# A fused attention and gated-MLP kernel on one core: the last projection in seven quads of seven products, and the second gate's weight blocks by way of a DRAM scratch

## The chip, the cores and the metric

The kernel runs on one core of a Trainium2 chip. The metric is device time in microseconds (us) for one execution. The engines are named as in the profile: PE multiplies matrices, DVE (vector), ACT (scalar) and POOL do elementwise work, SP issues transfers, and each works through its own queue in order. Matrix results land in eight PSUM banks of 128x512 numbers, which DVE and ACT read.

## The reference, cut to what matters

Two layers on a sequence of 2048 tokens of width 1024. The first (a chunked attention) is untouched by the change. The second is this:

```python
def _B_ref(x, w_in, w_sp, b_sp, w_out):          # x: 2048 x 1024, F = 3584, Fh = 1792
    z = _gelu(x @ w_in)                          # w_in: 1024 x 3584
    z1 = z[..., :Fh]
    z2 = _layernorm(z[..., Fh:])
    g = einsum('ts,bsf->btf', w_sp, z2) + b_sp[None, :, None]   # w_sp: 2048 x 2048
    return einsum('bsf,fd->bsd', z1 * g, w_out)  # w_out: 1792 x 1024
h  = x + A(layernorm(x))
h2 = h + _B_ref(layernorm(h), ...)
```

The product of `w_sp` and `z2` is called the gate. The product with `w_out` is the last projection; its result is added to `h`.

## The kernel before

The program is written as one long list of operations per engine. A small recorder (`_Recorder`, all operations issued at line L210) derives the semaphore waits between engines from the addresses that operations read and write. So the order on each engine is the order of the Python code, and nothing is rescheduled.

Several products are made by Strassen's scheme in Winograd's form: a product of 2x2 blocks by seven block products in place of eight, with sums of blocks on DVE ahead of them and sums of results afterwards. `SUMS` names the four derived weight blocks t1 to t4: t1 = b12 - b11, t2 = b22 - t1, t3 = b22 - b12, t4 = b21 - t2.

The part that matters here is the last third, from about 483 us on.

- **First gate**, `gate(0, ...)`: output tokens 0 to 1023. Seven groups g = 0 to 6. A group is seven products of eight matmuls of 128x512 each (names t2, t1, b11 for a later group, t3, b21, t4, b22 in the order on PE). The products t2, t3 and t4 pile up in one bank, and between them DVE must read the sum so far (`u2` after t2, `u3` after t3, `VB` after t4), so t3 waits for `u2` and t4 waits for `u3`. Between those reads DVE also makes the four sums `SS` for the next products (`s_sum`). `copy1` (ACT) takes b11's product to `s1`, and POOL adds the bias rows (`s1b2`, `s1b1`). The callbacks `each(g, k)` place other work at four points of a group.
- **Plain units**: 16 of them between the gates. A unit is 14 matmuls with `w_out` for 128 tokens by 512 columns, one addition on DVE (`fin`) and a store. They cover tokens 0 to 1023, which the first gate has just finished. Meanwhile 16 transposing transfers bring the second gate's blocks of `w_sp` (`sp_load(1, ...)`), DVE scales them to 16-bit floats and forms t1 to t4, and ACT takes sums of squares for the scales.
- **Second gate**, `gate(1, each=each1)`: tokens 1024 to 2047. Its `each1` places the work on the blocks of `w_out` (`ob_scale` on ACT, 16 `ob_sum` pieces on DVE).
- **Last projection in quads**: four groups, each seven products of seven matmuls for two chunks of 128 tokens by 1024 columns, that is what four plain units do. They cover tokens 1024 to 2047.

Of the kernel before, what the change touches and what calls it, by code (L numbers as in the profile page):

```python
# [33 lines left out]
class _Recorder:  # L34
# [52 lines left out]
    def record(self, eng, name, args, kw, dma=None):  # L87
# [94 lines left out]
        if dma is not None:  # L182
            self.dmas.append(op)
            if any(self.cells_of(a)[0] == "dram" for a in aps_out):
                self.out_dmas.append(op)
            sb = [a for a in aps_out + aps_in if self.cells_of(a)[0] == "sbuf"][0]
            key = (aps_out[0] is sb, sb.tensor.name, int(sb.offset))
            sem = self.dma_sems.get(key)
            if sem is None:
                sem = self.dma_sems[key] = [self.nc.alloc_semaphore("d%d" % len(self.dma_sems)), 0]  # L190
            sem[1] += 16
            op.val = sem[1]
            op.dma = sem[0]
# [65 lines left out]
def bass_sequential_preLN__memory_aug_infini_attn__mixer_gmlp__prompt_kernel(  # L259
# [141 lines left out]
    SQB = b3("sqb", [128, 28], BF16)  # L401
# [13 lines left out]
    WO1 = [tens("w_out1%d" % i, [128, 7, 512], BF16, o * K) for i, o in enumerate((30, 190))]  # L415
    WO0H = [tens("w_out0h%d" % i, [128, 7, 512], F16, o * K) for i, o in enumerate((54, 198))]
    FIN2 = tens("fin2", [128, 4, 2, 2, 512], BF16, 14 * K)
    OT4 = [[tens("ot%d%d" % (i, k), [128, 512], F32, (o + 2 * k) * K) for k in range(4)] for i, o in enumerate((38, 118))]
    SY = [tens("sy%d" % i, [128, 4, 7, 128], F16, o * K) for i, o in enumerate((4, 126))]
    FIN = [tens("fin%d" % i, [128, 512], BF16, o * K) for i, o in enumerate((37, 197, 12, 13))]  # L420
# [765 lines left out]

    def sp_load(pr, k, j):
        r0, c0 = 1024 * pr + (512 if k in ("b12", "b22") else 0), 1024 if k in ("b21", "b22") else 0
        sp.dma_start_transpose(RAW[k][:, :, j * 128:(j + 1) * 128],
                               B_w_sp[r0 + j * 128:r0 + (j + 1) * 128, c0:c0 + 1024])  # L1190
# [29 lines left out]
    def prod(b, a, w, first):  # L1220
        for i in range(8):
            pe.matmul(bank(b), a[:, i, :], BH[w][:, i, :], start=(first and i == 0), stop=(i == 7),
                      skip_group_check=True)

    def gate(pr, seam=lambda: None, mid=lambda: None, each=lambda g, k: None):
        inv, zo = (INV[0], Z1T) if pr == 0 else (INVY, Z1X)
        t1, t2 = slice(1024 * pr, 1024 * pr + 512), slice(1024 * pr + 512, 1024 * pr + 1024)
        s1, s1b1, s1b2, u2, u3 = (TMP[k][:] for k in ("s1", "s1b1", "s1b2", "u2", "u3"))
# [26 lines left out]
        pool.tensor_tensor(s1b2, s1, BROW[1][:], ALU.add)  # L1255
        pool.tensor_tensor(s1b1, s1, BROW[0][:], ALU.add)
        p1(1)
        if not pr:
            p1(2)
# [3 lines left out]
        for g in range(7):  # L1263
# [10 lines left out]
            if 1 - pr <= g <= 3:  # L1274
                p1(g + 2)
# [160 lines left out]
    for i in range(2):  # L1436
        sp.dma_start(WO0[i][:], wout[:, 7 * i:7 * i + 7, 0:512])

    units = [(tc, 0, 512) for tc in range(6)] + [(tc, 512, 512) for tc in range(8)] + [(tc, 0, 512) for tc in (6, 7)]
# [8 lines left out]

    def z1_norm(g, k):
        for h in range(k and 2):  # L1450
            r, o = 2 * g + (k > 2), 1024 + 512 * h
            if k != 2:
                act.activation(bank(7), Z1T[:, r, o:o + 512], ACTF.Square, accum_out=SQY[:, 2 * r + h:2 * r + h + 1])

    gate(0, seam, mid, z1_norm)
    pool.tensor_copy(TW[:], TOT[:])
    fin_load(units[0], act)
    fin_load(units[1], act)
    for k in ("b11", "b12", "b22", "b21"):
        for j in range(4):  # L1460
            sp_load(1, k, j)
    brow_load(1, act)
    for i in range(2):
        act.dma_start(WO1[i][:], wout[:, 7 * i:7 * i + 7, 512:D])
    pool.tensor_copy(SQB[:], SQY[:])

    def total(n):
        b = next_bank()
        pe.matmul(PS[:, b, 0:n], ONES[:], SQB[:, 0:n], start=True, stop=True)
        dve.tensor_reduce(out=TOT[:], in_=PS[:, b, 0:n], axis=mybir.AxisListType.X, op=ALU.add)  # L1470
        dve.tensor_single_scalar(TOT[:], TOT[:], 1e-30, ALU.max)
# [6 lines left out]
    def scale_y():  # L1478
        total(28)
        pool.tensor_single_scalar(TW[:], TW[:], float(2 * T * FH), ALU.mult)  # L1480
        for k in range(2):
            pool.tensor_tensor(TW[:], TW[:], BSQ[:, k:k + 1], ALU.add)
        pool.tensor_tensor(TOT[:], TOT[:], TW[:], ALU.mult)
# [5 lines left out]
    def brow_sq():  # L1489
        for k in range(2):  # L1490
            act.activation(BH["t4"][:, k, :], BROW[k][:], ACTF.Square, scale=float(np.sqrt(2.0)), accum_out=BSQ[:, k:k + 1])

    def wo_norm(k):
        v = (WO0, WO1)[k // 4][k // 2 % 2].rearrange("p c n -> p (c n)")[:, 1792 * (k % 2):1792 * (k % 2) + 1792]
        act.activation(BH["t4"][:, 0:4, :].rearrange("p c n -> p (c n)")[:, 0:1792], v, ACTF.Square, accum_out=SQY[:, k:k + 1])

    def scale_w():
        total(8)
        power(SCW)
        dve.tensor_tensor(INVO[:], YS[:], SCW[:], ALU.mult)  # L1500
        dve.reciprocal(INVO[:], INVO[:])

    for n, u in enumerate(units):
        if n + 2 < 16:
            fin_load(units[n + 2], act)
        out_unit(u, (lambda i: WO0[i // 7][:, i % 7, :]) if u[1] == 0 else
                 (lambda i: WO1[i // 7][:, i % 7, :]), act)
        if 1 <= n <= 8:
            wo_norm(n - 1)
        if n == 6:  # L1510
            brow_sq()
        if n == 7:
            scale_y()
        if n == 10:
            pool.tensor_copy(SQB[:, 0:8], SQY[:, 0:8])
        if n == 1:
            sp_half("b11")
        if n == 4:
            sp_half("b12")
            sp_sum("t1")  # L1520
        if n == 6:
            sp_half("b22")
            sp_sum("t3")
        if n == 8:
            sp_sum("t2")
        if n == 10:
            sp_half("b21")
            sp_sum("t4")
        if n == 12:
            scale_w()  # L1530
        if n == 13:
            for k in range(1, 4):
                s_sum(k, 0)

    OB = {"b11": WO0H[0], "b21": WO0H[1], "b12": Z1X[:, 0:7, 0:512], "b22": Z1X[:, 7:14, 0:512],
          "t1": Z1X[:, 0:7, 512:1024], "t2": Z1X[:, 7:14, 512:1024], "t3": Z1X[:, 0:7, 0:512]}

    def ob(k, i):
        if k == "t4":
            return Z2H[:, 4 * (i % 4):4 * (i % 4) + 4, 896 * (i // 4):896 * (i // 4) + 128]  # L1540
        return OB[k][:, i, :]

    def ob_scale(k, h):
        src = {"b11": WO0[0], "b21": WO0[1], "b12": Z1T[:, 0:7, 0:512], "b22": Z1T[:, 7:14, 0:512]}[k]
        s = slice(4 * h, 4 + 3 * h)
        act.activation(OB[k][:, s, :], src[:, s, :], ACTF.Copy, scale=SCW[:])

    def ob_sum(o, h):
        a, b = SUMS[o]
        s = slice(h, min(h + 2, 7))  # L1550
        if o == "t4":
            n = 4 * (s.stop - s.start)
            t = 4 * (h % 4)
            dve.tensor_tensor(Z2H[:, t:t + n, 896 * (h // 4):896 * (h // 4) + 128].rearrange("p (c m) n -> p c m n", m=4),
                              OB[a][:, s, :].rearrange("p c (m n) -> p c m n", m=4),
                              OB[b][:, s, :].rearrange("p c (m n) -> p c m n", m=4), ALU.subtract)
            return
        dve.tensor_tensor(OB[o][:, s, :], OB[a][:, s, :], OB[b][:, s, :], ALU.subtract)

    def y_blk(i, j, g, lo=0, hi=7):  # L1560
        t = 1024 + 512 * i + 128 * g
        return Z1X[:, 7 * j + lo:7 * j + hi, t:t + 128]

    def y_sum(k, g, lo=0, hi=7):
        y = SY[g % 2]
        o = y[:, k - 1, lo:hi, :]
        a, b, op = {1: (y_blk(1, 0, g, lo, hi), y_blk(1, 1, g, lo, hi), ALU.add),
                    2: (y[:, 0, lo:hi, :], y_blk(0, 0, g, lo, hi), ALU.subtract),
                    3: (y_blk(0, 0, g, lo, hi), y_blk(1, 0, g, lo, hi), ALU.subtract),
                    4: (y_blk(0, 1, g, lo, hi), y[:, 1, lo:hi, :], ALU.subtract)}[k]  # L1570
        (pool if lo else dve).tensor_tensor(o, a, b, op)

    def fin_in(g):
        for i in range(2):
            tc = 8 + 4 * i + g
            sp.dma_start(FIN2[:, g, i, :, :], out2d[tc * 128:(tc + 1) * 128, :].rearrange("p (h n) -> p h n", h=2))

    def fin_out(g, i, j, lo=0, hi=512):
        tc = 8 + 4 * i + g
        sp.dma_start(out2d[tc * 128:(tc + 1) * 128, 512 * j + lo:512 * j + hi], FIN2[:, g, i, j, lo:hi])  # L1580

    def each1(g, k):
        jobs = {(0, 0): [(ob_scale, "b11", 0)], (0, 1): [(ob_scale, "b11", 1)], (0, 2): [(ob_scale, "b12", 0)],
                (0, 3): [(ob_scale, "b12", 1)], (1, 0): [(ob_scale, "b22", 0)], (1, 1): [(ob_scale, "b22", 1)],
# [49 lines left out]
    for x in range(1, 4):  # L1634
        y_sum(x, 0, 6, 7)
# [69 lines left out]
```

## Time and profile before

| what | value |
|---|---|
| median of 3 runs | 747.42 us (746.77 to 747.52) |
| the profiled execution's own time | 747.58 us |
| its span in the profile | 745.9 us |
| PE busy | 738.8 us, 99% of the span |
| DVE, ACT, POOL busy | 595.8, 439.4, 296.1 us |
| granted PE clock | 1.0 all through |

How to read it: the span is from the first to the last instruction of the profiled execution; 1.7 us lie around it. Busy PE time includes overlap of matmuls that follow each other, so what a matmul costs is read from start to start. Times inside the trace count from the span's start. A row of the timeline gives start, duration, engine, line, operation, output and inputs, shape and count, and in brackets how long the engine sat idle before and what released it.

### The profile page before, as it was taken

To read this page: it belongs to the slowest core of one execution; us is meant where nothing else is said; L and a number is where in the kernel's file an instruction comes from. 1 tells how busy PE (TensorE), PEld (TensorE's weight loads), DVE (VectorE), ACT (ScalarE), POOL (GpSimd) and SP (SyncE) were. 2 spreads that over 40 slices of the span, in tenths; PEclk is the share of its full clock that TensorE was granted. 3 is DMA by queue.
4 is the path that set the end of the run, shared out by engine and by line. 5 is a ranking of instruction groups with operands and counts; after the bars stand their busy time and mean duration, and the time that the engine had idled before them with its cause. 6 is when DMAs were issued, how large, how long until landed. Compare 5 with 4: busy or idle time off the path is not lost.

```text
span 745.9 us, 13501 instructions
## 1 busy us (share of the span) xinstructions
PE 738.8 (99%) x5419; PEld 353.9 (47%) x5419; DVE 595.8 (80%) x1041; ACT 439.4 (59%) x567; POOL 296.1 (40%) x443
## 2 busy tenths in 40 slices
PE   8999999999999999999999999999999999999998
PEld 4445555445545445545554444444444444444444
DVE  5587889899988989878896777797774485989776
ACT  6777888888887888726876669823330445300000
POOL 2565456555554344110155899531220011222342
PEclk9999999999999999999999999999999999999999
DMA  9655668466645752744050036320029960001211
GB/s 298 178 169 128 139 143 176 128 154 157 172 104 166 244 172 64 180 112 128 29 141 1 1 61 123 75 82 0 1 41 162 238 207 18 1 1 52 68 50 56
DMA packets 139374, 82.41 MB, mean 110 GB/s; under 512 B 98352, under 2 KB 126768, under 8 KB 139312
## 3 DMA queue, kind: packets, MB, share of 16 engines
q1 hardware_dynamic: 131776, 74.48, 39.1%
q10 hardware_dynamic: 7536, 7.08, 3.5%
q8 instruction: 42, 0.69, 0.4%
q14 instruction: 20, 0.16, 0.1%
HBM read 50.08 MB, written 8.39 MB: 78 GB/s over the span
## 4 chain that ended last, share of the span: by engine, by line
PE 93%; DVE 4%; ACT 1%; DMA 1%; issue 0%; POOL 0%; DVEq 0%
PE ps L210 93%; DVE sqz L210 1%; DMA wv<-in_A_wv_dram 1%; DVE stats L210 1%; ACT e L210 0%; DVE hch L210 0%; POOL sz L210 0%; DVE tm L210 0%; DVE otok L210 0%; DVE sq L210 0%; DVE rdm L210 0%; DVE pqk L210 0%; DVE rd L210 0%; DVE etmp L210 0%; ACT qk L210 0%
## 5 line engine op out<-in xcount | busy, mean ns | idle before, releaser
L210 ACT ACTIVATE e<-ps 128x2048 bf16<-128x2048 f32 (+1 forms) x96 | 152.7, 1590 | 21.3 <-PE ps L210 20.6
L210 POOL TENSOR_SCALAR_AFFINE_SELECT e<-e 128x512 bf16<-128x512 bf16 x128 | 90.9, 723 | 123.4 <-ACT e L210 123.2
L210 POOL TENSOR_TENSOR tmp_s1b<-tmp_s,brow 128x512 f32<-128x512 f32 x28 | 36.5, 1306 | 121.7 <-DVE tmp_u L210 63.4
L210 PE MATMUL ps<-xnT,wk 128*128 128x512 bf16 x256 | 60.8, 380 | 0.6 <-ACT v L210 0.4
L210 PE MATMUL ps<-wv,xnT 128*128 128x512 bf16 x256 | 60.0, 381 | 0.7 <-DMA wv<-in_A_wv_dram 0.7
L210 PE MATMUL ps<-xnT,wq 128*128 128x512 bf16 x256 | 60.5, 379 | 0.0
L210 PE MATMUL ps<-wo,oT 128*128 128x512 bf16 x256 | 58.2, 380 | 0.8 <-DVE hch L210 0.8
L210 PE MATMUL ps<-w_out,z1T 128*128 128x512 bf16 x224 | 48.6, 379 | 0.0
L210 PEld LDWEIGHTS ps<-v,e 128*128 128x128 bf16 x1280 | 38.8, 96 | 14.0 <-issue 6.5
L210 ACT ACTIVATE tmp_s<-ps,invy 128x512 f32<-128x512 f32 x7 | 4.8, 687 | 64.0 <-POOL tmp_s1b L210 36.0
L210 PE MATMUL ps<-v,e 128*128 128x33 bf16 x1280 | 42.2, 178 | 0.0
L210 POOL TENSOR_TENSOR sz<-wzh 128x512 f16<-128x512 f16 x28 | 34.0, 1216 | 11.2 <-PE ps L210 11.2
L210 DVE BATCH_NORM_STATS2 zst<-z 128x6 f32<-128x448 bf16 x64 | 38.0, 609 | 0.0
L210 PEld LDWEIGHTS ps<-wo,oT 128*128 128x128 bf16 x256 | 24.0, 98 | 28.6 <-DVE hch L210 1.3
L210 PEld LDWEIGHTS ps<-xnT,wk 128*128 128x128 bf16 x256 | 22.6, 98 | 30.6 <-issue 4.5
L210 DVE TENSOR_TENSOR zt<-ps,zt 128x512 f32<-128x512 f32 x28 | 19.1, 686 | 22.2 <-PE ps L210 19.3
L210 ACT ACTIVATE qk<-ps 128x512 bf16<-128x512 f32 x48 | 28.7, 599 | 12.9 <-PE ps L210 12.9
L210 PEld LDWEIGHTS ps<-wv,xnT 128*128 128x128 bf16 x256 | 23.2, 98 | 27.7 <-DMA wv<-in_A_wv_dram 0.9
L210 PE MATMUL ps<-qk 32*128 32x128 bf16 (+3 forms) x512 | 34.5, 302 | 0.7 <-DVE tm L210 0.5
L210 ACT ACTIVATE tmp_s<-ps,inv 128x512 f32<-128x512 f32 x7 | 4.8, 687 | 50.9 <-POOL tmp_s1b L210 37.9
L210 PEld LDWEIGHTS ps<-xnT,wq 128*128 128x128 bf16 x256 | 23.5, 98 | 22.9 <-issue 0.2
L210 PEld LDWEIGHTS ps<-w_out,z1T 128*128 128x128 bf16 x224 | 21.7, 98 | 26.2
(259 smaller groups left out, 1651.0 us busy)
## 6 DMA issues: line engine op xcount, KB each, us to landing
nb<-in_B_w_in_dram SPq DMA_DIRECT2D x16, 448.0 KB, 4.0
nb<-in_B_w_sp_dram SPq DMA_DIRECT2D x14, 512.0 KB, 4.6
xch<-in_A_x_dram SPq DMA_DIRECT2D x16, 256.0 KB, 4.3
xr<-in_A_x_dram SPq DMA_DIRECT2D x16, 256.0 KB, 4.0
out_dram<-hch SPq DMA_DIRECT2D x16, 256.0 KB, 2.4
wz<-in_B_w_in_dram SPq DMA_DIRECT2D x6, 512.0 KB, 4.6
wo<-in_A_wo_dram SPq DMA_DIRECT2D x1, 2048.0 KB, 8.5
fin<-out_dram ACTq DMA_DIRECT2D x16, 128.0 KB, 3.1
```

What stands on the lines that cost most here:

```text
L210: ins = getattr(e, op.name)(*op.args, **op.kw)
```

## The change

Eight groups of four units' work make up the last projection (2048 tokens by 1024 columns). Before, 16 plain units and four quads did it. After, four plain units (tokens 0 to 255) and seven quads do it: quads 0 to 2 take tokens 256 to 1023, quads 3 to 6 take tokens 1024 to 2047, all behind the second gate. For this the first gate's output for tokens 256 to 1023 is scaled and turned into 16-bit floats on ACT during the second gate, after a sum of squares over it (`y0_norm`, `y0_scale`, `y0_conv`).

The second gate's `w_sp` blocks are transposed during the first gate into six staging tiles, stored to a DRAM tensor `WSPT`, and read back by four plain loads of 1 MB (`q_load`). ACT converts b11, b12 and half of b21, DVE b22 and the other half. The sums of squares over `w_out` and over the first gate's operand move into the first gate. In the second gate the first two bias additions move from POOL to DVE, `ob_load` brings blocks of `w_out` in pieces of 128 columns, and the block sums of `w_out` are placed in other groups.

```diff
+    STG = [tens("stg%d" % i, [128, 8, 128], BF16, o * K) for i, o in enumerate((54, 56, 58, 198, 200, 202))]
+    WSPT = nc.dram_tensor("w_spT", (4, 128, 4, 1024), BF16, kind="Internal").ap()
+    HOME1 = {"b11": 4, "b12": 118, "b22": 46, "b21": 126, "t1": 38, "t2": 22, "t3": 118, "t4": 14}
...
+    def stage_in(n):
+        sp.dma_start_transpose(STG[n % 6][:], sp_rows(1, Q4[n // 4], n % 4))
+    def stage_out(n):
+        sp.dma_start(WSPT[n // 4, :, n % 4, :], STG[n % 6][:].rearrange("p c n -> p (c n)"))
+    def q_load(k):
+        sp.dma_start(RAW1[k][:].rearrange("p j c n -> p j (c n)"), WSPT[Q4.index(k)])
+    def q_conv(k):
+        if k == "b22":
+            dve.tensor_single_scalar(BH1[k][:], RAW1[k][:], SC[0][:], ALU.mult)
+            return
+        if k == "b21":
+            dve.tensor_single_scalar(BH1[k][:, 0:2], RAW1[k][:, 0:2], SC[0][:], ALU.mult)
+        for r in range(2 * (k == "b21"), 4):
+            act.activation(BH1[k][:, r], RAW1[k][:, r], ACTF.Copy, scale=SC[0][:])
+    def q_sum(o):
+        a, b = SUMS[o]
+        dve.tensor_tensor(BH1[o][:], BH1[a][:], BH1[b][:], ALU.subtract)
...
-        pool.tensor_tensor(s1b2, s1, BROW[1][:], ALU.add)
-        pool.tensor_tensor(s1b1, s1, BROW[0][:], ALU.add)
+        for o, k in ((s1b2, 1), (s1b1, 0)):
+            (dve if pr else pool).tensor_tensor(o, s1, BROW[k][:], ALU.add)
         p1(1)
-        if not pr:
-            p1(2)
+        p1(2)
...
+    for n in range(20):
+        if n < 16:
+            stage_in(n)
+        if n >= 4:
+            stage_out(n - 4)
+    w0_load(1)
-    units = [(tc, 0, 512) for tc in range(6)] + [(tc, 512, 512) for tc in range(8)] + [(tc, 0, 512) for tc in (6, 7)]
+    units = [(tc, 512 * h, 512) for h in range(2) for tc in range(2)]
...
+    def each0(g, k):
+        z1_norm(g, k)
+        for h, lo in ((1, 15), (0, 21)):
+            for n in range(14):
+                if 4 * g + k == lo + n // 5:
+                    w_norm(h, n)
+            if 4 * g + k == lo + 2 and h:
+                w0_load(0)
...
+        if (g, k) == (4, 0):
+            total(28, SQY, TOTY)
+        if (g, k) == (6, 0):
+            brow_in(1)
+            q_load("b11")
+            q_load("b12")
+            q_conv("b11")
+        if (g, k) == (6, 1):
+            fin_load(units[1])
+            w1_load(1)
+            q_conv("b12")
+        if (g, k) == (6, 2):
+            brow_in(0)
+            fin_load(units[2])
+            fin_load(units[3])
+    gate(0, seam, mid, each0)
+    q_load("b22")
+    q_load("b21")
...
+    brow_sq()
+    q_sum("t1")
     for n, u in enumerate(units):
...
+        if n == 0:
+            s_sum(1, 0)
+            s_sum(2, 0)
+        if n == 2:
+            scale_y()
+            q_conv("b21")
+            q_sum("t3")
         if n == 1:
+            q_conv("b22")
+    q_sum("t2")
+    s_sum(3, 0)
...
+    NG = 7
+    def tcs(g):
+        return (2 + g, 5 + g) if g < 3 else (5 + g, 9 + g)
...
+    for r in range(14):
+        job(r // 7, (r % 7) // 2, y0_norm, r)
+    for h in range(4):
+        job(2 + (h + 1) // 4, (h + 1) % 4, y0_conv, h)
+        job(3 + (h + 1) // 4, (h + 1) % 4, y_sum, h + 1, 0)
+    job(2, 0, y0_scale)
+    job(0, 0, q_sum, "t4")
+    job(0, 0, scale_w)
+    for r in range(7):
+        job(1, 0, ob_load, "b12", r)
+        job(3, 0, ob_load, "b22", r)
...
+    slots = [(2, 1), (2, 2), (2, 3), (3, 0)] + [(g, k) for g in range(4, 7) for k in range(4)][1:12]
+    for n, (o, h) in enumerate([(o, h) for o in ("t1", "t2", "t3", "t4") for h in range(4)]):
+        if n < len(slots):
+            job(*slots[n], ob_sum, o, h)
...
-    for g in range(4):
+    ob_sum("t4", 3)
+    for g in range(NG):
```

`total(n, src)` puts one small matmul on PE and two small operations on DVE; `power` is one POOL operation and two on DVE. `brow_sq` squares the two bias rows on ACT, `scale_y` scales them. `job(g, k, ...)` puts work at point k of group g of the second gate.

## The prediction

> **What bounds the kernel now.** I read the page first (busy shares, then the chain that ended last), then PE's timeline from the first gate on, then DVE's and ACT's in the same stretch, last the stretches of DMA.
>
> ```profile
> PE 738.8 (99%) x5419; PEld 353.9 (47%) x5419; DVE 595.8 (80%) x1041; ACT 439.4 (59%) x567; POOL 296.1 (40%) x443
> ...
> PE 93%; DVE 4%; ACT 1%; DMA 1%; issue 0%; POOL 0%; DVEq 0%
> ```
>
> PE is never free: a matmul removed is time removed, unless PE then waits for another engine. PE's timeline prices the matmul:
>
> ```profile
> 565.79 1.89 PE L210 MATMUL ps<-b22h,ss 128*128 128x512 f16 x8
> 567.51 24.34 PE L210 MATMUL ps<-w_out,z1T 128*128 128x512 bf16 x112
> 591.69 0.18 PE L210 MATMUL ps<-sqb,ones 128*128 128x28 bf16 x1
> 591.72 15.27 PE L210 MATMUL ps<-w_out,z1T 128*128 128x512 bf16 x70
> ```
>
> 112 matmuls from 567.51 to 591.69 are 0.216 us each; a gate product of eight is 1.726 us from start to start (565.79 to 567.51). The tiny matmul with ones costs PE some 0.03 us. From 482 us on PE shows one late start, 0.08 us:
>
> ```profile
> 674.43 1.28 DVE L210 TENSOR_TENSOR z1x<-z1x 128x1024 f16<-128x1024 f16 x2
> 675.63 0.74 DVE L210 SCALAR_TENSOR_TENSOR tmp_u<-ps,invy,tmp_s1b 128x512 f32<-128x512 f32 x1
> ...
> 674.62 1.89 PE L210 MATMUL ps<-b21h,z2h 128*128 128x512 f16 x8
> 676.43 1.90 PE L210 MATMUL ps<-t4h,z2h 128*128 128x512 f16 x8
> ```
>
> This is the second gate's group 4: two `ob_sum` pieces stand ahead of `u3`, so t4 starts at 676.43 and not at 676.35, 0.06 us after `u3` ends. DVE is the engine that PE will meet when work is moved.
>
> **The gain.** Plain units go from 16 to 4, 12 x 14 = 168 matmuls less; quads from 4 to 7, 3 x 49 = 147 more. 21 matmuls x 0.216 = 4.53 us. The new operands with a stride (four runs of 128 columns) cost nothing extra: the last projection's t4 already reads in such runs, seven matmuls in 1.51 us.
>
> **The staging.** 16 transposes (1.4 us of SP each: four in 5.50) and 16 stores of 256 KB, some 0.75 us of DMA each (at the 335 GB/s shown below), start when the first gate does. At 2.2 us a step they end near 519, with SP's later loads queued behind them; `w_out` lands some 6 us later, near 525. Its first reader is ACT's `w_norm`, which cannot start before 527.8 (`copy1` at 525.65, then two squares). Ten of these at 0.755 us end at 535.3; PE asks for them at 539.9 (`total` writes the bank that the squares use). Price nothing, with 2 us of cover at the load and 4.6 at the matmul; beyond that PE waits one for one. The squares moved into the first gate lie in ACT's idle time (8.5 us ahead of each `copy1`).
>
> **The seam between the gates** is the dear place. Before, 48.4 us of units covered it; now 12.1. A chain begins at 553.90 with ACT's last `copy1` and has no gap:
>
> ```profile
> 553.90 0.69 ACT L210 ACTIVATE tmp_s<-ps,inv 128x512 f32<-128x512 f32 x1 [12.60 <-PE ps L210]
> 554.49 0.59 ACT L210 ACTIVATE ps<-z1T 128x512 f32<-128x512 bf16 x1
> 555.23 0.60 ACT L210 ACTIVATE ps<-z1T 128x512 f32<-128x512 bf16 x1
> ...
> 592.02 2.29 DVE L210 TENSOR_TENSOR t1h<-b12h,b11h 128x4096 f16<-128x4096 f16 x1
> 594.23 1.28 DVE L210 TENSOR_TENSOR fin<-fin,ps 128x512 bf16<-128x512 bf16 x2
> 595.42 1.28 DVE L210 TENSOR_SCALAR b22h<-b22r,sc 128x4096 f16<-128x4096 bf16 x1
> ```
>
> On ACT: `copy1` 0.59 (start to start), 14 `w_norm` at 0.755 = 10.57, eight conversions of 128x1024 (1.14 each in the trace, 1.04 start to start) 8.32, the last one's end 0.10: b12 is ready at 573.5. On DVE from there, from start to start: t1 2.21, fin 0.60, two sums 1.33, fin 0.60, b22 1.31, fin 0.60, the scale's three small ones 0.46, half of b21 0.64, t3 2.21, fin 0.60, t2 2.21, a sum 0.60, the two bias additions 1.28, c11 and its product 1.24, `u2` 0.67, a sum 0.61, t4 2.21, the scale of `w_out` 1.28 (as from 611.88 to 613.16, a trip to POOL in it), `u3` 0.75 and 0.06 to PE. That is 21.47: PE may start t4 of group 0 at 595.0. PE's own work brings it there at 553.70 (`p1(6)`'s end) + eight products 13.81 + units 12.09 + four products 6.90 + four more 6.90 + 0.03 = 593.4. So PE waits 1.57 us here (part of it at t3, for `u2`). The bias additions moved from POOL have no row on DVE; 0.60 to 0.75 each from the f32 additions there, 0.64 taken. Bounds for the seam: 0 (the chain's starts 1.6 earlier in all, over its 40 operations) and 3 (1.5 later). Queued behind `u3` on DVE are `VB` and the next `SS` sums; PE's b22 wants the first, and has 1.7 us for it.
>
> **The second gate.** A group's DVE work is 9.1 us: PE has 12.08 in groups 1 to 3, 10.36 in the others. After t2's end `u3` may start 4.38 us later where no b11 product stands between (three products 5.18, less `u3`'s 0.75 and 0.06), 6.1 with one; else t4 is late.
>
> - Group 2: `y0_scale` has DVE wait for PE's `total`, 3.70 after t2's end. It takes 2.04 (1.66 as from 611.88 to 613.54, and a second pair of small ones 0.38), then one `ob_sum` 0.60: `u3` at 6.34, t4 0.2 late.
> - Group 4: from `u3` to the next `u2` DVE takes 6.45 (675.63 to 682.08). Two `y_sum` pieces there in group 3 put group 4's `u2` at 0.87 after t2's end instead of 0.20. Then, from start to start, `u2` 0.67, sums 0.61, 0.72 and 0.61, `y_sum` 0.60, `ob_sum` 0.60: `u3` at 4.68, t4 0.30 late.
> - Group 5: two `ob_sum` make those 6.45 into 7.65; with 0.81 to PE that is 8.46, where t3 was due 0.81 + 6.90 = 7.71 after the same `u3`: 0.75 late. One and a half more pieces ahead of `u3` put t4 0.09 late. Group 6 has no sums for a next group and makes it up.
>
> Together 1.34 us, bounds 0.4 (today's late start, five times) and 3 (each piece twice as dear). The quads' `sy` addition takes 0.61 alone and 1.58 beside POOL's additions, but POOL's in the gate run beside `VB` reads and end before the next piece. [...]
>
> ACT: 14 `y0_norm` of about 1 us, `ob_scale` (1.99 and 1.56) and eight `y0_conv` pieces of about 1.3 (from the rows of 1024 and 1536) end near 628, 1.4 us ahead of the `y_sum` that wants them; beyond that DVE and PE wait. The 14 `ob_load` of 128 KB go out from 591 on; at the transposes' 180 GB/s seven take 5 us, and ACT asks at 611. Price nothing.
>
> **The quads** add three groups of the form already there, where DVE idles 1.7 us ahead of `u3`'s counterpart; nothing waits.
>
> **The sum.** -4.53 - 0.08 (today's late start, counted anew above) + 0.03 (three `total` for two) + 1.57 + 1.34 = -1.67. From the profiled execution's 747.58 that is 745.9; it lies 0.16 above the median of the runs, 747.42, so 745.8 is my time.
>
> **The rivals.**
>
> *A, all covered.* DVE and ACT keep their places and the gain comes whole: 747.42 - 4.5 = 742.9. For it: hand sums from start to start are tight and small overlaps may help. Against: the seam's chain has no gap and the one late start today is of just this kind.
>
> *B, slower: the scratch comes back late.* From 559.1 (when t2's old block, b11's new home, is free) to the end of b21 one queue holds 5.64 MB: four blocks 4.19, `w_out` 0.92, bias rows and `fin` 0.53. DVE wants b21 at 580.6, 7.1 us into its chain. Two stretches give the rate:
>
> ```profile
> 570.00:573.00 3.00, 3.00 (x16) 1.36 (x14) 0.69 (x1) 0.00 (x0) 0.00 (x0) 1.00 1.22 214
> 601.00:602.00 1.00, 1.00 (x6) 0.48 (x5) 0.00 (x0) 1.00 (x1) 0.78 (x3) 1.00 0.99 335
> ```
>
> (PE, PEld, DVE, ACT, POOL busy, clock, DMA share, GB/s.) Plain loads run at 335, loads among transposes at 214. Data flow some 1.5 us after an issue. At 335 all is in at 559.1 + 1.5 + 16.8 = 577.4; at 214 at 587.0, 6.4 us late, and PE as much: 752.2. It turns slower than before by 0.2% where b21 lands 3.1 us late, at a rate of about 244. For it: 1 KB pieces of bias and `w_out` lie between. Against: no transposes are in that queue.
>
> The profile shows the clock at 1.0 in every stretch. [...]
>
> *C, no change.* The second gate's jobs at their upper bound, 3 us in place of 1.34, the seam as forecast: 747.5.
>
> *Not doing what it says* is excluded for PE: the order of instructions holds 56 unit matmuls and 343 in quads.
>
> **How the numbers follow.** A measurement of this kernel tells about 0.2% (1.5 us) from no change, so my forecast lies on that edge: chance 0.47 for it, of which 0.27 is faster by over 0.2% and 0.20 within. A 0.20 (faster), B 0.20 (slower), C 0.13 (within). Faster 0.47, same 0.33, slower 0.20. The range goes from A's time, 742.9, to 749.0, the lower half of B; the forecast's own is 744.3 to 747.3.
>
> **What would show it.** Right: 56 unit matmuls in one piece of 12.1 us, PE's late starts at t4 of the second gate's group 0 (1.3 to 1.6 us, released by `tmp_u`) and at t3 and t4 of groups 4 and 5, none in the quads. The first step falls if ACT's b12 conversion ends elsewhere than about 6 us after the first gate, the second if DVE idles ahead of group 5's `u2`. Wrong: b21's conversion waiting for DMA, PE waiting at `total` in the first gate, or a clock under 1.0.

## The result, and the profile after

| | before | after |
|---|---|---|
| median of 20 runs each, side by side | 747.79 us (746.77 to 748.95) | 746.46 us (745.68 to 747.40) |
| the profiled execution's own time | 747.58 us | 747.36 us |
| its span | 745.9 us | 745.6 us |
| from the first gate's first matmul to the last product's first | 258.52 us | 256.94 us |
| granted PE clock | 1.0 all through | 1.0 all through |

The ratio of the times is 0.9982 [0.9975, 0.9989]: 1.33 us, or 0.18%, faster. The two profiled executions differ by 0.22 us only. That is chance at the start: after's first gate begins at 483.90 instead of 482.91, with the same instructions in front of it, and over all profiles of this study that moment lies between 482.26 and 483.90. So each kernel is judged below by the fourth row, here called the stretch: 1.58 us less.

The profile's page of after, PE's busy time and the chain that ended last:

```profile
PE 735.0 (99%) x5399; PEld 351.4 (47%) x5399; DVE 609.9 (82%) x1065; ACT 480.5 (64%) x656; POOL 307.7 (41%) x448
...
PE 84%; DVE 7%; ACT 3%; issue 3%; DMA 1%; POOL 1%; ACTq 0%; DVEq 0%; POOLq 0%
```

There are 20 PE instructions fewer (21 matmuls less, one `total` more). PE had 93% of the chain before and has 84% now: other engines now decide in places. PE's timeline shows where (start, duration, operation, and in brackets the idle time and its releaser):

```profile
568.54 12.25 PE L214 MATMUL ps<-w_out,z1T 128*128 128x512 bf16 x56
...
595.54 1.90 PE L214 MATMUL ps<-t4g,z2h 128*128 128x512 f16 x8 [0.92 <-DVE tmp_u L214]
...
649.82 1.90 PE L214 MATMUL ps<-t3g,ss 128*128 128x512 f16 x8 [0.44 <-DVE tmp_u L214]
...
667.35 1.67 PE L214 MATMUL ps<-w_out0h,z1x 128*128 128x512 f16 x7
669.81 1.69 PE L214 MATMUL ps<-w_out0h,z1x 128*128 128x512 f16 x7 [0.78 <-ACT ot L214]
```

The units are one piece, as they should be. A start is late by the time since the start of the product before it, less that product's 1.726 us (1.51 for seven matmuls). That gives 1.07 us at t4 of group 0 (due 594.47), 0.05 and 0.04 at t4 of groups 2 and 4, 0.60 and 0.06 at t3 and t4 of group 5, 0.16 at t3 of group 6, and 0.95 at quad 0's b21 product. Together 2.93 us. With the terms of the prediction's sum that are no waits, -4.53 - 0.08 + 0.03 + 2.93 = -1.65, beside the measured -1.58.

At the first place DVE's timeline shows the end of the chain that the prediction followed:

```profile
574.37 2.29 DVE L214 TENSOR_TENSOR t1g<-b12g,b11g 128x4096 f16<-128x4096 f16 x1 [4.36 <-ACT b12g L214]
...
594.43 0.15 DVE L214 TENSOR_SCALAR top<-top 128x1 int32<-128x1 int32 x1 [0.67 <-POOL top L214]
...
594.73 0.75 DVE L214 SCALAR_TENSOR_TENSOR tmp_u<-ps,invy,tmp_s1b 128x512 f32<-128x512 f32 x1
```

From t1 to PE's start it takes 21.17 us, and DVE idles in it once, 0.67 us for POOL in the scale of `w_out`.

The scratch came back in time. The DMA view of 555 to 600 us (issue, count, size, time to landing) and a window of the same stretch (PE, PEld, DVE, ACT, POOL busy, clock, DMA share, GB/s):

```profile
b21q<-w_spT SPq DMA_DIRECT2D x1, 1024.0 KB, 8.6
```

```profile
570.00:573.00 3.00, 3.00 (x15) 1.36 (x14) 0.01 (x1) 3.00 (x4) 0.00 (x0) 1.00 1.11 395
```

b21 was issued at 569.10, so it landed at 577.7; DVE read it at 581.35.

### The profile page after: what moved, and what is told of

Same layout as the page of the kernel before. It is cut to its first block, busy times and chain, and to the rows that moved or that the text cites. A ratio compares the mean times of both kernels' runs of the same rounds, so it can differ in the third digit from the quotient of the medians.

```text
span 745.6 us, 13617 instructions
## 1 busy us (share of the span) xinstructions
PE 735.0 (99%) x5399; PEld 351.4 (47%) x5399; DVE 609.9 (82%) x1065; ACT 480.5 (64%) x656; POOL 307.7 (41%) x448
## 4 chain that ended last, share of the span: by engine, by line
PE 84%; DVE 7%; ACT 3%; issue 3%; DMA 1%; POOL 1%; ACTq 0%; DVEq 0%; POOLq 0%
PE ps L214 84%; ACT ps L214 1%; DMA wv<-in_A_wv_dram 1%; DVE sqz L214 1%; DVE vb L214 1%; DVE stats L214 1%; ACT b12g L214 1%; DVE tmp_u L214 0%; ACT b11g L214 0%; DVE ss L214 0%; DVE z1x L214 0%; ACT e L214 0%; DVE hch L214 0%; POOL sz L214 0%; DVE tm L214 0%
## 5 line engine op out<-in xcount | busy, mean ns | idle before, releaser
L214 POOL TENSOR_TENSOR tmp_s1b<-tmp_s,brow 128x512 f32<-128x512 f32 x26 | 33.9, 1305 | 104.5 <-DVE tmp_u L214 37.0
L214 ACT ACTIVATE ot<-ps,invo 128x512 f32<-128x512 f32 x7 | 4.8, 687 | 70.6 <-PE ps L214 70.6
L214 POOL TENSOR_TENSOR ot<-ot,fin 128x512 f32<-128x512 f32 x21 | 27.9, 1352 | 47.1 <-ACT ot L214 47.1
L214 PE MATMUL ps<-z2h,sy 128*128 128x512 f16 (+2 forms) x182 | 37.4, 363 | 0.0
L214 ACT ACTIVATE z<-zp,inv 128x448 bf16<-128x448 f32 x28 | 18.6, 665 | 19.5 <-DVE zp L214 19.4
```

What stands on the lines that cost most here:

```text
L214: ins = getattr(e, op.name)(*op.args, **op.kw)
```

## The experiments

All are edits of the changed kernel. Times stand against the kernel before in the same comparison.

**The scale of `w_out` ahead of the chain.** `scale_w` (one small matmul, four small DVE operations and a trip to POOL between them) goes from group 0 of the second gate to the end of the first.

```diff
+    scale_w()
     brow_sq()
...
-    job(0, 0, scale_w)
```

> The scale of w_out (five small operations on DVE, POOL and PE, 1.33 us of DVE in the second gate's group 0) is made right after the first gate, where DVE sits idle for 4.4 us. Theory (the seam is one chain, ACT to DVE to PE, with no gap): u3 of group 0 starts 1.3 us earlier, the wait of 1.07 us at t4 goes to nothing, time 1.07 us under the changed kernel's. Rival (PE waits there for the loads or for POOL): the wait stays at 1.07.

745.43 us, ratio 0.9967 [0.9954, 0.9979]; the stretch is 255.85, 1.09 less than after's. t4 of group 0 starts on time, the other waits are unchanged. The wait at the seam is the DVE chain's, and it is worth its full 1.07 us.

**The pieces of `w_out`'s sums elsewhere.** Group 4 keeps one `ob_sum`, group 6 takes six.

```diff
-    slots = [(2, 1), (2, 2), (2, 3), (3, 0)] + [(g, k) for g in range(4, 7) for k in range(4)][1:12]
+    slots = [(2, 1), (2, 2), (2, 3), (3, 0), (4, 1), (5, 0), (5, 1), (5, 2), (5, 3),
+             (6, 0), (6, 0), (6, 1), (6, 1), (6, 2), (6, 3)]
```

> The sums of w_out blocks in groups 4 to 6 of the second gate are placed otherwise: one in group 4, four in group 5, six in group 6, where DVE has no sums for a next group. Theory (DVE falls behind because two pieces stand between u3 and the next u2 in group 4): t3 of group 5 is no longer 0.60 us late and t3 of group 6 no longer 0.16; some 0.7 us less. Rival (ACT's blocks or POOL's additions hold DVE): the late starts stay.

745.34 us, ratio 0.9968 [0.9956, 0.9981]; stretch 256.18, 0.76 less. t3 of groups 5 and 6 is on time, t4 of group 5 0.08 late. So 0.60 + 0.16 were the price of the pieces' places.

**A cover for quad 0's b21 product.** Quad 0's products go b11, b21, t2, t1, t3 and so on. b11 and b21 pile up in one bank: ACT copies b11's product out of it (`ot`), then b21 is added and DVE reads the sum (c11). t2, t3 and t4 pile up in another, which DVE reads after t2 (f12) before t3 may start. ACT's timeline of after, then PE's of before:

```profile
669.06 0.69 ACT L214 ACTIVATE ot<-ps,invo 128x512 f32<-128x512 f32 x1 [14.89 <-PE ps L214]
```

```profile
702.13 1.46 PE L210 MATMUL ps<-z1x,sy 128*128 128x512 f16 x6
703.42 1.67 PE L210 MATMUL ps<-w_out0h,z1x 128*128 128x512 f16 x7
```

Before, six t2 matmuls (702.13) stood between b11 (700.62) and b21 (703.42), while ACT copied (702.33 to 703.02). In after nothing stands between b11 and b21 (667.35 and 669.81 above). In this experiment quad 0's t2 product is put there, as a cover (work that hides a wait).

```diff
     o_adds(0)
+    o_prod(3, sy(2, 0), "t2", True)
     o_p2(0)
...
-        o_prod(bb, sy(2, g), "t2", True)
+        if g:
+            o_prod(bb, sy(2, g), "t2", True)
```

> In the changed kernel the first quad's b21 product follows its b11 product at once, and PE sits 0.95 us until ACT has copied the bank out. Here the t2 product (seven matmuls, 1.51 us) stands between them, as it did before the change. Theory (the wait is ACT's read of the bank): b21 starts on time, nothing else moves, and the stretch of PE from the first gate's first product to the last quad's last products goes from 256.94 us to 256.0; time 0.95 us under the changed kernel's, 1.3 + 0.95 = 2.3 us under before. Rival (the copy is late because POOL, DVE or the blocks of w_out are late): the wait only moves one product on, and the time stays.

746.46 us, ratio 0.9982 [0.9973, 0.9991]: no gain over after; the stretch is 256.82. PE's timeline and DVE's of this kernel:

```profile
670.00 1.67 PE L214 MATMUL ps<-w_out0h,z1x 128*128 128x512 f16 x7
...
673.83 1.69 PE L214 MATMUL ps<-z2h,z1x 128*128 128x512 f16 x7 [0.65 <-DVE ot L214]
```

```profile
671.71 0.75 DVE L214 SCALAR_TENSOR_TENSOR fin<-ps,invo,fin 128x512 bf16<-128x512 f32 x1 [2.65 <-PE ps L214]
672.38 0.73 DVE L214 TENSOR_TENSOR z2h<-w_out0h,z2h 128x512 f16<-128x512 f16 x1
673.04 0.74 DVE L214 SCALAR_TENSOR_TENSOR ot<-ps,invo,ot 128x512 f32<-128x512 f32 x1
```

b21 starts on time at 670.00. But t3 is now 0.81 late: it needs f12's read (`ot`, 673.04), and in front of that DVE does c11 and the last piece of t4, both queued there by the program's order. One wait had hidden another, and the time stayed.

**The same with DVE's order changed too.** c11 goes behind f12's read, the last t4 piece ahead of the quads.

```diff
+    slots.append((6, 3))
...
     o_adds(0)
+    o_prod(3, sy(2, 0), "t2", True)
     o_p2(0)
-    o_c11(0)
-    ob_sum("t4", 3)
...
-        o_prod(bb, sy(2, g), "t2", True)
+        if g:
+            o_prod(bb, sy(2, g), "t2", True)
...
         o_stt(g, f12[:], bb, f12[:])
+        if not g:
+            o_c11(0)
```

> As the first experiment, with t2 between the first quad's b11 and b21, but DVE's order follows: the first read of the bank (f12) stands ahead of c11, and the last piece of t4 is made before the quads. In the first experiment the wait only moved on: t3 was 0.81 us late, because f12 stood behind c11 and that piece on DVE. Theory now (two waits stood one behind the other, ACT's read and DVE's order): with both taken away the quads have no late start, the stretch goes from 256.94 to about 256.0, time 0.95 us under the changed kernel's. Rival (POOL's additions hold the quads' opening): f12 waits for POOL, and t3 stays late.

745.65 us, ratio 0.9971 [0.996, 0.9981]; stretch 255.99, 0.95 less. PE's timeline has no gap here any more, and t1 and t3 are one piece:

```profile
669.95 1.67 PE L214 MATMUL ps<-w_out0h,z1x 128*128 128x512 f16 x7
671.46 3.19 PE L214 MATMUL ps<-z2h,z1x 128*128 128x512 f16 x14
```

The rival's late t3 did not come: t3 follows t1 without a gap (14 matmuls in one piece from 671.46). Whether f12 waited for POOL is not shown.

**The bias additions back on POOL.** The prediction charged DVE's chain with the two bias additions that the change took from POOL.

```diff
-            (dve if pr else pool).tensor_tensor(o, s1, BROW[k][:], ALU.add)
+            pool.tensor_tensor(o, s1, BROW[k][:], ALU.add)
```

> The second gate's first two bias additions go back from DVE to POOL; DVE's chain through the seam is 1.21 us shorter. Theory (DVE's chain sets t4 of group 0, POOL has time): POOL starts them when ACT's copy ends, some 585.3, is done by 588, ahead of u2; the wait of 1.07 us at t4 goes, time 1.0 us under the changed kernel's. Rival (POOL's additions and DVE's large sums hinder each other, as the quads' 0.61 against 1.58 shows): what DVE is spared it loses on t2 (2.2 us) or t4 beside POOL, and the wait stays near 1.

746.66 us, ratio 0.998 [0.9971, 0.9988]; stretch 256.87, t4 of group 0 1.01 late: nothing won. POOL's timeline and DVE's show why:

```profile
585.08 4.33 POOL L214 TENSOR_TENSOR tmp_s1b<-tmp_s,brow 128x512 f32<-128x512 f32 x2 [7.04 <-ACT tmp_s L214]
```

```profile
586.75 1.64 DVE L214 TENSOR_TENSOR ss<-z2h 128x1024 f16<-128x1024 f16 x1
```

The pair took 2.27 on POOL in the kernel before (618.60); here it takes 4.33. DVE's sum beside it takes 1.64 instead of 0.68. DVE is rid of 1.21 us and loses 0.96 on that one sum, and most of the rest (0.18) on the product that follows the read of c11, 0.60 in place of 0.42. This is the rival, at another sum than it named: t2 (584.55, 2.28 long) began before POOL and lost nothing.

**ACT's part of the chain 3 us later.** Four of the squares over `w_out` are done twice, ahead of b11's conversion; nothing else changes.

```diff
         if (g, k) == (6, 0):
+            for n in range(4):
+                w_norm(0, n)
             brow_in(1)
```

> ACT takes four of its squares of w_out a second time ahead of the conversion of b11 (4 x 0.755 = 3.0 us). Theory (the chain through the seam begins on ACT): everything on it moves by 3.0 us, PE's late start at t4 of group 0 (with those ahead of it) goes from 1.07 to 4.1, time 3.0 us over the changed kernel's. Rival (the scratch's loads set the seam; b21 landed 3.6 us ahead of its reader): ACT's time is free, and the time stays.

750.25 us, ratio 1.0031 [1.0019, 1.0043]; stretch 260.59, 3.65 more. The chain is real, but it bit elsewhere. PE's timeline, then ACT's:

```profile
587.81 3.49 PE L214 MATMUL ps<-b21g,z2h 128*128 128x512 f16 x8 [2.36 <-ACT tmp_s L214]
591.13 1.89 PE L214 MATMUL ps<-t2g,ss 128*128 128x512 f16 x8
```

```profile
585.01 2.17 ACT L214 ACTIVATE b21g<-b21q,sc 128x1024 f16<-128x1024 bf16 x2
587.08 0.67 ACT L214 ACTIVATE tmp_s<-ps,invy 128x512 f32<-128x512 f32 x1
```

Group 0's b21 product adds to the bank that `copy1` reads, and `copy1` queues on ACT behind the bias rows' scaling, which waits for DVE's scale, and behind half of b21's conversion. In after, `copy1` starts at 584.59 and ends at 585.26, 0.5 us ahead of PE's b21 at 585.80. 3.02 us later less 0.5 is the 2.52 measured. So the chain meets PE in two places: at b21 with 0.5 us of cover, at t4 with none. The second part of the loss is in the windows (columns as above):

```profile
586.00:588.00 2.00, 0.19 (x1) 0.13 (x2) 2.00 (x3) 2.00 (x4) 0.00 (x0) 0.91 0.03 8
588.00:590.00 2.00, 2.00 (x6) 0.69 (x5) 2.00 (x2) 1.51 (x4) 0.00 (x0) 0.50 0.19 66
590.00:592.00 2.00, 2.00 (x9) 0.76 (x8) 2.00 (x4) 0.57 (x1) 0.00 (x0) 0.74 0.32 73
```

After the pause the clock is at half (0.50 from 588 to 590), and the b21 product takes 3.32 us from start to start, 1.59 more than 1.726. t4 is 0.61 late. 2.52 + 1.59 + 0.61 = 4.72, less after's 1.07 = 3.65.

Half clock is not worth its whole 1.59 in time, though. At full clock t4 would still wait for the chain, 3.02 us later than in after, so PE would lose 4.09 in place of 4.72 (worked out, not run). The six executions agree: the two whose mean clock is 1.0 took 749.69 and 749.85 us, the three at 0.997 took 750.48 to 750.69.

**No scratch.** The second gate's blocks come by four transposes each into place, when the plain loads would have gone out; the staging is left out.

```diff
     def q_load(k):
-        sp.dma_start(RAW1[k][:].rearrange("p j c n -> p j (c n)"), WSPT[Q4.index(k)])
+        for j in range(4):
+            sp.dma_start_transpose(RAW1[k][:, j], sp_rows(1, k, j))
...
-    for n in range(20):
-        if n < 16:
-            stage_in(n)
-        if n >= 4:
-            stage_out(n - 4)
```

> No DRAM scratch: the second gate's blocks come by 16 transposing transfers straight into place, where the changed kernel has its four loads; the staging in the first gate is gone. Theory (the scratch is what makes four units enough): SP needs 1.4 us for each transpose, so b22 is issued some 5 us and b21 some 10 us later, b21 lands near 588 where DVE asks at 581.4; PE waits 5 to 7 us more, with some more for a clock under 1.0, time near 752.5, slower than before. Rival (units and ACT's chain cover the transposes): within 1.5 us of the changed kernel.

752.55 us, ratio 1.0059 [1.0043, 1.0075]; stretch 263.93, 6.99 more than after's. PE's, DVE's and SP's timelines:

```profile
576.43 4.71 PE L214 MATMUL ps<-w_out,z1T 128*128 128x512 bf16 x21 [1.09 <-DMA w_out<-in_B_w_out_dram]
...
589.87 3.57 PE L214 MATMUL ps<-b21g,z2h 128*128 128x512 f16 x8 [3.37 <-ACT tmp_s L214]
```

```profile
582.66 1.29 DVE L214 TENSOR_SCALAR b22g<-b22q,sc 128x4096 f16<-128x4096 bf16 x1 [4.35 <-DMA b22q<-in_B_w_sp_dram]
...
590.87 2.29 DVE L214 TENSOR_TENSOR t2g<-b22g,t1g 128x4096 f16<-128x4096 f16 x1 [1.51 <-DMA out_dram<-fin]
```

```profile
580.01 5.67 SPq L214 DMA_TRANSPOSE b21q<-in_B_w_sp_dram  x4
```

b21's transposes go out from 580.01, where the plain load had landed at 577.7. PE's losses: a unit waits 1.26 for `w_out` in the same queue; the b21 product 3.72, through `copy1` again; half clock costs it 1.66 more; t4 is 1.34 late instead of 1.07. Together 6.91.

What they add up to is set by DVE's chain, for which t4 waits at the end. From t1 to t4 it takes 28.12 us (573.49 to 601.61) where after's takes 21.17, and DVE waits in it 4.35 for b22, 0.82 for b21 and 1.51 for a store that SP issues behind the transposes, but never for PE. So a full clock would have won nothing here; t4 would have waited the longer (worked out, not run). This is rival B's mechanism (the blocks late on one queue), brought about on purpose, and what the scratch is worth here: 7.0 us of the stretch.

**The three that gained, together** (`scale_w` early, the pieces' places, the quads' order):

> The quads' order of the run beside this, the early scale and the moved pieces of w_out in one kernel. Theory (three separate places, which add up): 0.95 + 1.09 + 0.76 = 2.8 us under the changed kernel's, the stretch about 254.1 us, time 743.7, so nearly all of the 4.53 us of the 21 matmuls; what is left of late starts is under 0.3. Rival (one wait gone brings the next engine's, as at the quad): less than 2 us under the changed kernel's.

743.66 us (743.45 to 743.91), ratio 0.9943 [0.993, 0.9956], span 741.9: 4.17 us faster than before and 2.8 faster than after. PE's timeline:

```profile
593.55 1.89 PE L214 MATMUL ps<-t4g,z2h 128*128 128x512 f16 x8
...
647.22 1.89 PE L214 MATMUL ps<-t3g,ss 128*128 128x512 f16 x8
```

0.17 us of late starts are left (t4 of groups 2, 4 and 5). The stretch is 254.12; the three edits alone had saved 1.09 + 0.76 + 0.95 = 2.80, together 2.82.

## Why the prediction was right, and where it was not

**The time.** 745.8 was forecast, 746.46 measured; the change forecast was -1.67, the measured -1.33 by the medians and -1.58 by the stretch. The largest term stood; the waits came out right in sum (2.93, forecast 2.91), but not in their places. That agreement is luck: the two terms that were forecast came to 1.98, 0.93 too large, and the one put at nothing came to 0.95.

**The gain** of 4.53 us is shown by the three edits together, where the waits are gone: 258.52 to 254.12 is -4.40, and without its 0.17 of late starts, today's 0.08 and the extra `total` it is -4.52. Strided operands cost nothing: seven matmuls of a quad take 1.51 us in after too.

**The seam**, the step "PE waits 1.57 us here", was over-sized: 1.07. Its place and kind were right. The chain from `copy1` to PE took 40.62 us (554.92 to 595.54), where the terms of the sum come to 41.05: ACT's part was 0.13 shorter (19.45 to t1's start), DVE's 0.30 shorter, by small overlaps (0.35 from the start of c11's product to `u2`, for one). That its end is DVE's and that the wait goes with 1.33 us of DVE's work is shown by the experiment with `scale_w`.

**The second gate**, "together 1.34 us", measured 0.91: group 2 0.05 (0.2 forecast), group 4 0.04 (0.30), group 5 0.60 and 0.06 (0.75 and 0.09), group 6 0.16 (none). One cause of the excess can be read off: each piece was priced at 0.60, but a `y_sum` takes 0.53 from start to start (640.36 to 640.89) and the last piece of each block, half as wide, 0.34 (629.11 to 629.45). Group 6's wait followed group 5's: both went when the pieces were moved.

**The quads**, "nothing waits", is the step that failed: 0.95 us, against the sign "none in the quads". The prediction looked at DVE ahead of `u3`'s counterpart only and took "groups of the form already there" for the first group too. Before, quad 0's b21 stood behind six t2 matmuls, which covered ACT's read of its bank (the rows of 702.13 and 703.42); the change took the six away. That ACT's read was the first of two waits, DVE's order the second, is shown by the two experiments there.

**The staging**, "price nothing", held, but with less cover than said. A step took 2.8 us in the mean and not 2.2 (the sixth transpose went out at 490.02, the last, ten steps on, at 517.78). A transpose waits for an older store out of its staging tile; SP stood 8.1 us for such stores, in ten waits, and they were slow (the DMA issues of after's page):

```profile
w_spT<-stg SPq DMA_DIRECT2D x16, 256.0 KB, 4.2
```

`w_out` was issued at 525.58, and ACT waited for it (its timeline):

```profile
531.83 0.60 ACT L214 ACTIVATE ps<-w_out 128x512 f32<-128x512 bf16 x1 [3.12 <-DMA w_out<-in_B_w_out_dram]
```

The forecast was 527.8, which is 528.8 by this execution's first gate. So the 2 us of cover at the load were gone, and ACT stood 3.12 us. PE did not feel it: the ten squares ended at 539.34, PE asked at 540.88, with 1.5 us of cover left of 4.6. `y0_conv` ended at 628.44, and DVE asked at 629.45: 1.0 for the 1.4 forecast.

**The rivals.** A, all covered, was refuted for this order of operations: 2.93 us of waits. But its price was right: the version without them saves 4.17 us by the medians, for 4.5 forecast. B, the scratch late, was refuted: the queue moved 395 GB/s in the window shown, above the 335 taken, and DVE had 3.6 us to spare. C, the pieces at twice their price, was refuted: 0.60 or less.

**DVE beside POOL, and the clock.** The prediction had POOL's additions end before the next piece, and they did: in after's timelines no piece of groups 4 and 5 ran beside a POOL instruction (the one at 648.42 begins 0.20 us after POOL's addition of 646.82 ends). Such overlaps did cost where they occurred: 0.96 us in the experiment with POOL's bias additions, and as much once in after. On POOL's timeline and on DVE's:

```profile
654.25 1.29 POOL L214 TENSOR_TENSOR tmp_s1b<-tmp_s,brow 128x512 f32<-128x512 f32 x1 [6.03 <-ACT tmp_s L214]
```

```profile
654.45 1.64 DVE L214 TENSOR_TENSOR ss<-z2h 128x1024 f16<-128x1024 f16 x1
```

POOL began first and DVE's sum took 0.96 more than the 0.68 of the same sum at 650.28. In the kernel before the same two began the other way round: DVE's sum at 687.73 took 0.69, POOL's addition at 687.77 took 1.66, not the 1.16 of the one at 676.46. In these two pairs most of the extra time fell on the one that began later (POOL's, in the first pair, took 1.29); so the price of an overlap has to be looked up instruction by instruction.

The clock played no part in after: it was 1.0 all through, and in the stretch no start is more than 1.07 us late. In the two kernels where b21 started 2.52 and 3.72 us late, half clock made that product 1.59 and 1.66 us longer. Of the time it cost less, worked out and not run: about 0.6 us with ACT later and nothing without the scratch, since t4 would have waited for DVE instead.

## What to carry to other kernels

When work moves into a place that was covered before, list every point where the chain meets the bottleneck engine, with its cover: here t4 (none) and group 0's b21 (0.5 us), and by itself the first quad's b21, whose cover the change removed. The first group of a repeated form is not like the others: ask which instruction stood in front of it, and look behind a wait for the next one before pricing its removal. And when the gain is a sum of removed work that is certain and waits that depend on order, moving small operations can win back more than the change itself brought: here a scale of 1.33 us, a few block sums and one product gave 2.82 us of the stretch, the change 1.58.

## What the runs showed of the hardware

In the run with ACT later, b11's last matmul ended at about 585.45 and the clock fell at about 587.64, some 2.2 us on (the window 586 to 588 has 0.91: 0.36 us of it at half); it was back at about 591.05, 3.4 us after the fall. Without the scratch the clock fell at about 589.88, some 3.4 us after PE's last matmul (586.50), and stayed at half for 3.4 us too, to about 593.29 (the window 590 to 592 has 0.50). So the two falls came after pauses of 2.2 and 3.4 us; what sets that time is not shown. Two of the six executions with ACT later, the same program, show a mean clock of 1.0.

The scratch's stores of 256 KB took 4.2 us to land beside transposes; 16 stores of the same size earlier in the program (`hch`) took 2.4 on the same page.
